# Storing the turned halves of x pair by pair, and two buffers for the gathered rows, in an attention and mixture-of-experts kernel

## The chip, the cores and the metric

The kernel runs on one core of one Trainium2 chip. The time is device microseconds of one execution; three executions of the kernel before were timed, and one more was profiled. PE is the matrix engine (TensorE), DVE the vector engine, ACT the scalar engine, POOL is GpSimd, SP issues most DMAs. A pair is two attention heads of one batch; there are 16 pairs, four for each of four batches.

## The reference

```python
def _attn_ref(q, k, v, centroids):          # q, k, v: 4 x 8 x 768 x 64
    q_assign = argmax(normed q . normed centroids)      # 16 clusters a head
    k_assign = argmax(normed k . normed centroids)
    mask = q_assign[:, :, :, None] == k_assign[:, :, None, :]
    scores = np.where(mask, scale * np.matmul(q, k.T), -1e9)
    ...
    return np.matmul(softmax(scores), v)

def _moe_ref(x, w_gate, w_noise, noise, w1, w2):        # x: 3072 x 512, 8 experts, F = 1024
    noisy_logits = x @ w_gate + log1p(exp(x @ w_noise)) * noise
    top2, top2_w = two largest a row, softmax of the two
    for e in range(E):
        for k in range(2):
            mask = top2[:, k] == e
            out[mask] += top2_w[mask, k, None] * (np.maximum(x[mask] @ w1[e], 0) @ w2[e])

x = attn_out.transpose(0, 2, 1, 3).reshape(B * S, H * D)   # attention's output is the experts' input
```

## The kernel before

One program does both parts. Attention goes pair by pair; a pair has 12 steps, and a hand-written table `AT` with due times in steps says where in that sequence every smaller piece of work is put. `at(step, f, ...)` files a piece under a third of a step; the loop over `t` in `attention` then calls, for each step, the pieces of the first third, `scores`, `split_p`, the second third, `values`, and the last third. The order in which Python calls them is the order of each engine's instructions: every engine works through its own list in order, and waits by semaphores.

In a step PE makes scores (L518), ACT takes the exponent (L519, tile `pe`), POOL splits it (L530, tile `pl`; for the last pairs DVE does that), and PE multiplies with v (L547 to L553). Beside it run, for the pairs behind, the maxima over keys (`b_max`: PE L487, DVE L490) and the cluster choice (DVE L425 to L442, the last of which writes the one-hot tile `oh`; PE turns it at L451, ACT makes the mask `mk`, SP places it). All PE results of this kind go through the PSUM tile `ring` with 6 buffers. `values` ends with DVE writing the pair's columns of the batch's output `xt` (L558 to L561; L558 reads `am`, L561 reads `rs`).

When the four pairs of a batch are done, two things happen for the whole batch within some five steps. `g_logits` and `g_logits2` turn `xt` on PE (L606), copy it on ACT (L608), multiply it with the gate's weights (L616) and copy that (L617); `g_turn` (PE L627, DVE L628) and `g_gate`, a chain of small DVE operations, choose the two experts of each token, and `g_list` writes the token into the table of its expert. And `store_x`, three times for two of the six token groups each, splits `xt` into two half-precision parts (ACT L598, then DVE L599 with two inputs in SBUF) in tile `xh`, which has one buffer, and SP stores them to `xs` in DRAM (L600): 128 pieces of 4 KB. For the last batch these calls stand in `experts`, between pieces of the first expert's first layer.

`experts` takes eight experts with up to 832 tokens each, in seven tiles of 128 (the last of 64). `gather_x` (POOL, L1128) fetches a tile of rows of `xs`; `turn_x` (SP, L1137, a DMA transpose) turns it into `xT`, of which there is one buffer. `layer1` is PE L1146, with ACT L1032 and L1034 and DVE L1035 behind it, `layer2` PE L1183 (L1174 and L1177 for the last tile), and POOL scatters the result (L1196). Expert 0 starts with the tokens of the first three batches (four tiles, part A); its other three tiles (part Bs) come when the last batch has been gated (`l_hot`, `l_sum`) and stored. With `late=1` all eight column blocks of its `layer1` stand behind `g_turn`: four inside the gate's chain, four beside `l_hot`, `l_sum`, `split_w2` and `store_x`. In the later experts `gather_x` of the next expert's tiles 0 to 3 stands in front of `layer1`, and all of its turns, with the gathers of tiles 4 to 6, in `tail`, between the pieces of `layer2`. SP also loads the weights (`stg`, 7 buffers) in the order of its list.

Memory in SBUF is laid out by pool; within a pool each tile lies behind the one that was asked for before it, all buffers of a name together. Pool `mo` (the experts') is opened when attention's pools `wk` and `fix` are closed and starts where `wk` began; a tile waits for the last use of each tile that lay in its place. `wk` holds, in this order and in bytes a partition, each rounded up to 32: `mm` 2 x 48, `nt` 2 x 512, `am` 3 x 48, `pe` 6 x 3,072, `vv` 3 x 6,240, `pl` 5 x 1,536, `rs` 2 x 24, `xm`; `fix` lies behind it and begins with `A0`. `mo` holds `xT` 13,312, `hT` 24,576, `hE` 2,048, `w2t` 16,384, three lists (448, 224 and 224), and then the smaller tiles.

## Time and profile before

| | us |
|---|---|
| median of three runs | 1095.08 (1093.82 to 1095.15) |
| profiled execution, its own time | 1094.86 |
| its span, first to last instruction | 1092.6 |
| PE busy in it | 1013.3 (93%) |

The profile is a page with shares of busy time, a list of waits and DMA issues, and views of any stretch. A timeline row gives start, duration, engine, line, operation, tiles, and in brackets the idle time in front of it with what ended that. In the page's second part each digit is the busy share of one of 40 equal slices.

### The profile page before, as it was taken

To read this page: it belongs to the slowest core of one execution; us is meant where nothing else is said; L and a number is where in the kernel's file an instruction comes from. 1 tells how busy PE (TensorE), PEld (TensorE's weight loads), DVE (VectorE), ACT (ScalarE), POOL (GpSimd) and SP (SyncE) were. 2 spreads that over 40 slices of the span, in tenths; PEclk is the share of its full clock that TensorE was granted. 3 is DMA by queue.
4 is the path that set the end of the run, shared out by engine and by line. 5 is a ranking of instruction groups with operands and counts; after the bars stand their busy time and mean duration, and the time that the engine had idled before them with its cause. 6 is when DMAs were issued, how large, how long until landed. Compare 5 with 4: busy or idle time off the path is not lost.

```text
span 1092.6 us, 22148 instructions
## 1 busy us (share of the span) xinstructions
PE 1013.3 (93%) x8518; PEld 685.8 (63%) x8518; DVE 687.4 (63%) x1455; ACT 512.0 (47%) x1046; POOL 549.1 (50%) x598
## 2 busy tenths in 40 slices
PE   5789998999899998988998999999999999999994
PEld 4678896889778896875444545545455454554542
DVE  5787676887768786897836554556445564455511
ACT  3467766767576766665512523315223152241510
POOL 9267673789766893872143434224352343423211
PEclk9899998999999999999999999999999999999998
DMA  7776765666755663505078484473844748445200
GB/s 197 172 186 145 175 159 167 144 173 144 196 142 137 168 157 95 158 10 157 39 233 202 126 194 162 104 212 117 201 144 102 216 117 205 140 102 164 59 33 33
DMA packets 143247, 158.08 MB, mean 145 GB/s; under 512 B 68857, under 2 KB 120441, under 8 KB 143138
## 3 DMA queue, kind: packets, MB, share of 16 engines
q1 hardware_dynamic: 129842, 120.25, 43.5%
q0 software_dynamic: 13296, 36.38, 10.9%
q8 instruction: 68, 1.11, 0.4%
q14 instruction: 41, 0.34, 0.1%
HBM read 78.21 MB, written 26.51 MB: 96 GB/s over the span
## 4 chain that ended last, share of the span: by engine, by line
PE 63%; DVE 13%; issue 8%; DMA 7%; POOL 4%; SPq 2%; ACT 2%; POOLq 0%; DVEq 0%; ACTq 0%
PE ring L1146 19%; PE ring L1183 17%; PE ring L518 8%; PE ring L487 4%; DMA A<-mk 2%; DVE aux L490 2%; PE av L547 2%; PE av L553 2%; PE av L549 2%; DVE mm L490 2%; DMA xs<-xh 1%; PE ring L406 1%; PE ring L385 1%; DVE pl L530 1%; DVE xh L599 1%
## 5 line engine op out<-in xcount | busy, mean ns | idle before, releaser
L530 POOL TENSOR_TENSOR pl<-pe 128x768 f16<-128x768 f32 x173 | 253.4, 1479 | 102.5 <-ACT pe L519 100.0
L1146 PE MATMUL ring<-xT,w1t 128*128 128x416 f16 (+2 forms) x1536 | 274.8, 340 | 2.0 <-DMA xT<-xg 2.0
L1183 PE MATMUL ring<-w2t,hT 128*128 128x512 f16 x1152 | 253.8, 381 | 2.2 <-ACT w2t L1038 1.2
L519 ACT ACTIVATE pe<-ring,l 128x384 f32<-128x384 f32 x384 | 201.5, 578 | 66.9 <-PE ring L518 62.0
L1146 PEld LDWEIGHTS <-w1t 128*128 128x128 f16 x1536 | 149.9, 98 | 121.2 <-issue 4.6
L1183 PEld LDWEIGHTS <-hT 128*128 128x128 f16 x1152 | 112.7, 98 | 137.0 <-issue 4.9
L1032 ACT ACTIVATE hr<-ring 128x416 f32<-128x416 f32 (+2 forms) x128 | 66.6, 520 | 276.4 <-PE ring L1146 269.1
L1196 POOL DMA_INDIRECT out<-yo,idx x52 | 62.7, 1207 | 173.1 <-DVE yo L1192 112.9
L490 DVE TENSOR_REDUCE aux<-ring 128x1 f32<-128x384 f32 x192 | 107.9, 562 | 60.8 <-PE ring L487 53.5
L518 PE MATMUL ring<-A 128*128 128x384 f32 x384 | 142.0, 370 | 1.0 <-ACT pe L519 0.7
L1035 DVE TENSOR_TENSOR hT<-hr,hT 128x416 f16<-128x416 f32 (+3 forms) x128 | 71.5, 560 | 101.0 <-ACT hT L1034 90.2
L518 PE MATMUL ring<-B 128*128 128x384 f32 x384 | 130.0, 339 | 1.5 <-DMA B<-nt 1.5
L1128 POOL DMA_INDIRECT xg<-xs,idx x52 | 54.6, 1050 | 145.0 <-DMA xT<-xg 120.4
L487 PE MATMUL ring<-A 128*128 128x384 f32 x384 | 108.8, 357 | 17.1 <-ACT pe L519 6.9
L1192 DVE SCALAR_TENSOR_TENSOR yo<-ring,we,xt 128x512 f32<-128x512 f32 (+1 forms) x49 | 36.7, 748 | 124.3 <-PE ring L1183 103.9
L490 DVE TENSOR_REDUCE mm<-ring 128x1 f32<-128x384 f32 x192 | 105.0, 547 | 0.0
L547 PE MATMUL av<-vv,pe 128*128 128x65 f16 x1152 | 98.0, 195 | 1.8 <-DVE xt L561 1.2
L549 PE MATMUL av<-vv,pe 128*128 128x64 f16 x1152 | 97.0, 193 | 0.0
L547 PEld LDWEIGHTS <-pe 128*128 128x128 bf16 x1152 | 80.1, 99 | 17.3 <-issue 12.6
L487 PEld LDWEIGHTS ring<-A 128*128 128x128 f32 x384 | 69.4, 190 | 30.5 <-ACT pe L519 13.6
L549 PEld LDWEIGHTS <-pe 128*128 128x128 bf16 x1152 | 78.5, 99 | 0.4
L518 PEld LDWEIGHTS ring<-A 128*128 128x128 f32 x384 | 73.3, 191 | 2.7 <-ACT pe L519 1.2
(206 smaller groups left out, 1412.8 us busy)
## 6 DMA issues: line engine op xcount, KB each, us to landing
stg<-in_moe_w SPq DMA_DIRECT2D x64, 512.0 KB
A<-hl SPq DMA_DIRECT2D x30, 384.0 KB
B<-hl SPq DMA_DIRECT2D x30, 384.0 KB
vt<-in_v SPq DMA_DIRECT2D x8, 768.0 KB
out<-zt SPq DMA_DIRECT2D x12, 512.0 KB
xs<-xh SPq DMA_DIRECT2D x12, 512.0 KB
A<-hl SPq DMA_DIRECT2D x60, 96.0 KB
B<-hl SPq DMA_DIRECT2D x30, 192.0 KB
```

The lines of the kernel that those rows point to most:

```text
L487: nc.tensor.matmul(t, A[:, 0, s, j * 128:j * 128 + 128], A[:, 1, s, n * 384:n * 384 + 384], start=True, stop=True)
L490: nc.vector.tensor_reduce(o, t, axis=X, op=OP.max, negate=True)
L518: nc.tensor.matmul(t, M[:, 1 - qi, s, ks], M[:, qi, s, ns], start=not qi, stop=bool(qi))
L519: nc.scalar.activation(pe[:, n], t, AF.Exp, bias=self.l64[:, 0:1], scale=self.scale)
L530: (nc.vector if last else nc.gpsimd).tensor_tensor(lo, pe, hi, op=OP.subtract)
L547: nc.tensor.matmul(av[:, j, :], ph[:, js], vv[:, hh, kj, 64:129], start=(kc == 0 and j == 0), stop=False, skip_group_check=True)
L549: nc.tensor.matmul(av[:, j, :64], ph[:, js], vv[:, hh, kj, 0:64], start=False, stop=False, skip_group_check=True)
L1032: nc.scalar.activation(r[:, :n], p, AF.Relu, scale=2.0 ** -HT)
L1035: nc.vector.tensor_tensor(h1, r[:, a:b], h0, op=OP.subtract)
L1146: nc.tensor.matmul(p, self.w1t[:, wi, c, f * 128:f * 128 + 128], self.xT[:, xi, c, n0:n1], start=(i == 0), stop=(i == 3 * ND - 1))
L1183: nc.tensor.matmul(p, self.hT[:, hi, f, t * 128:t * 128 + 128], self.w2t[:, wi, f], start=(i == 0), stop=(i == 3 * NF - 1))
L1196: i = nc.gpsimd.indirect_dma_start(out=self.out, out_offset=bass.IndirectOffsetOnAxis(ap=en[:r], axis=0), in_=yo[:r], in_offset=None, boun ...
```

## The change

`store_x` now takes one pair's 128 columns of all six token groups, and is called for each pair soon after its last `values`: pieces of 768 columns instead of 1024, 16 instead of 12, stored as 768 pieces of 512 B. `xs` keeps a row for each token; within a row the halves now alternate in blocks of 128 columns. The pieces of pairs 0 to 12 are in attention, those of 13 to 15 in `experts`. `xT` gets two buffers and is first asked for in `turn_x`, so behind `hT`, `hE`, `w2t` and the lists in pool `mo`. Turns 0 to 3 of the next expert and gathers 4 to 6 move from `tail` into `layer1` of the expert in front (`prep_x`); for expert 1 the first four gathers move in front of the last part-A `layer2`. `late` is gone: column block 0 of expert 0's `layer1` stands in front of `g_logits`, and each `split_w2` of expert 0 one place earlier.

```diff
@@ attention @@
+            if p <= NP - 4:
+                at(w + 37 + L + (6 if p == 0 else 0), self.store_x, p)
...
-                for c in range(3):
-                    at(z + 1.333 + 1.333 * c, self.store_x, b, c)
@@ store_x @@
-        h = pool.tile([128, n, 2, self.DM], F16, name="xh")
-        x, s = self.xt[b][:, n * c:n * c + n], self.sx[:, b:b + 1]
+        h = pool.tile([128, NJ, 2, 128], F16, name="xh")
+        x, s = self.xt[b][:, :, 128 * c:128 * c + 128], self.sx[:, b:b + 1]
         self.nc.scalar.activation(h[:, :, 0], x, AF.Copy, scale=s)
         self.nc.vector.scalar_tensor_tensor(h[:, :, 1], x, s, h[:, :, 0], op0=OP.mult, op1=OP.subtract)
-        self.nc.sync.dma_start(rap(self.xs, b * 128 * W + V * c, [[W, 128], [1, V]]), h.rearrange("p j i c -> p (j i c)"))
+        self.nc.sync.dma_start(rap(self.xs, b * 128 * NJ * W + 256 * c, [[NJ * W, 128], [W, NJ], [1, 256]]),
+                               h.rearrange("p j i c -> p j (i c)"))
@@ experts @@
-        self.xT = mo.tile([128, 2, ND, CAP], F16, name="xT")
+        self.xT = {}
...
         for c in range(4):
             self.max_w2(0, c)
+        self.layer1(0, 0, [A])
         for j in range(NJ):
             self.g_logits(b, j)
...
-        if not late:
-            self.layer1(0, 0, [A])
         self.g_turn(b)
...
-        f = 0 if late else 1
+        f = 1
...
+        self.split_w2(0, 0)
         self.l_hot(0)
...
-            self.split_w2(0, i)
             if i < 3:
-                self.store_x(b, i)
+                self.split_w2(0, i + 1)
+            if i:
+                self.store_x(self.NP - 4 + i)
...
                 for i in range(TA, T):
                     self.turn_x(0, i)
+                for i in range(4):
+                    self.gather_x(1, i)
...
             self.prep_w2(1, f - 5)
+            self.prep_x(1, f - 3)
             self.layer1(0, f, [Bs])
...
                     self.prep_w1(e + 1, f - 3)
+                    self.prep_x(e + 1, f - 3)
                 self.layer1(e, f, [(0, n), (n, CAP)])
...
+    def prep_x(self, e, i):
+        if 0 <= i < 4:
+            self.turn_x(e, i)
+            if i + 4 < self.T:
+                self.gather_x(e, i + 4)
@@ tail @@
-        done = 0
+        done = 4
...
-                while done < T and done < (t + 3 if e else 4 * (t - t0 + 1)):
-                    self.turn_x(n, done)
-                    if done + 4 < T:
-                        self.gather_x(n, done + 4)
-                    done += 1
+            while n < E and done < min(T, (t if e else 2 * (t - t0)) + 5):
+                self.turn_x(n, done)
+                done += 1
@@ turn_x @@
+        if t == 0:
+            self.xT[e] = self.mo.tile([128, ND, 2, self.CAP], F16, name="xT", bufs=2)
```

## Rows read from the trace of the kernel before

**Rows 1.** The table of stretches (busy time of each engine, granted clock of PE as a share of full speed, DMA share, GB/s): the end of attention and the last batch's logits, the way to the second expert, experts 1 to 7.

```profile
506.40:516.05 9.65, 8.03 (x83) 4.92 (x80) 6.62 (x10) 4.88 (x12) 0.00 (x0) 0.82 0.70 117
516.05:596.70 80.65, 74.36 (x399) 38.13 (x397) 48.80 (x110) 27.63 (x56) 26.38 (x32) 0.98 0.54 144
596.70:1044.00 447.30, 447.30 (x2342) 227.20 (x2343) 235.02 (x388) 153.75 (x327) 159.57 (x224) 1.00 0.53 147
```

**Rows 2.** The same table for single pairs: the first pairs of batches 1 and 2 (in which the batch before is stored and its logits are made) with a mid-batch pair between them, and two shorter stretches after the ends of batches 0 and 2.

```profile
156.30:197.30 41.00, 36.36 (x434) 30.75 (x433) 25.02 (x58) 26.03 (x54) 18.90 (x14) 0.92 0.60 163
...
250.70:275.70 25.00, 24.33 (x322) 22.90 (x319) 19.34 (x46) 18.13 (x38) 24.04 (x26) 1.00 0.63 153
275.70:316.50 40.80, 34.21 (x434) 28.77 (x432) 26.71 (x58) 25.83 (x53) 22.92 (x20) 1.00 0.60 163
...
176.00:187.80 11.80, 9.11 (x89) 7.05 (x90) 6.02 (x12) 8.21 (x17) 2.94 (x2) 0.71 0.28 102
...
421.50:433.50 12.00, 11.10 (x132) 9.05 (x133) 8.24 (x19) 8.96 (x21) 3.96 (x4) 0.86 0.17 57
```

**Rows 3.** The view of the tile `xh`: the operations that write and store it (shortest, median and longest in ns), and what ACT waited for in front of its part.

```profile
L598 ACT ACTIVATE xh<-xt,sx x12: 1143/1147/1150, 167.5 to 543.7; 128x1024 f16<-128x1024 f32 x12
L599 DVE SCALAR_TENSOR_TENSOR xh<-xt,sx,xh x12: 1265/1284/3866, 168.9 to 544.9; 128x1024 f16<-128x1024 f32 x12
...
  DMA xs<-xh: 19.6, 8
```

**Rows 4.** The timeline of PE behind the three batch ends: the pieces with the long idle times, and two groups of the same four turns, one early and one late.

```profile
178.63 0.90 PE L385 MATMUL ring<-ident,qk 128*128 128x128 f32 x3 [3.65 <-ACT lg L617]
...
181.03 1.12 PE L606 MATMUL ring<-ident,xt 128*128 128x128 f32 x4
...
184.37 0.66 PE L606 MATMUL ring<-ident,xt 128*128 128x128 f32 x4
...
298.20 0.55 PE L385 MATMUL ring<-ident,qk 128*128 128x128 f32 x3 [2.57 <-ACT lg L617]
...
304.49 0.44 PE L487 MATMUL ring<-A 128*128 128x384 f32 x1 [2.11 <-ACT pe L519]
...
422.37 0.45 PE L487 MATMUL ring<-A 128*128 128x384 f32 x1 [1.72 <-ACT pe L519]
```

**Rows 5.** The timelines of POOL and of DVE around the first store of batch 1.

```profile
286.44 2.89 POOL L530 TENSOR_TENSOR pl<-pe 128x768 f16<-128x768 f32 x2
...
289.37 1.46 POOL L530 TENSOR_TENSOR pl<-pe 128x768 f16<-128x768 f32 x1
...
288.60 3.32 DVE L599 SCALAR_TENSOR_TENSOR xh<-xt,sx,xh 128x1024 f16<-128x1024 f32 x1
```

**Rows 6.** POOL, DVE and PE in a mid-batch pair, about the step in which the change puts a pair's store; then POOL and DVE at the same place of two others, the first and the last of the nine pairs of this kind.

```profile
261.68 2.90 POOL L530 TENSOR_TENSOR pl<-pe 128x768 f16<-128x768 f32 x2
...
261.86 0.56 DVE L442 TENSOR_TENSOR oh<-ring,km 128x384 bf16<-128x384 f32 x1
262.34 0.56 DVE L490 TENSOR_REDUCE aux<-ring 128x1 f32<-128x384 f32 x1
...
263.58 0.52 PE L487 MATMUL ring<-A 128*128 128x384 f32 x2
...
115.52 1.47 POOL L530 TENSOR_TENSOR pl<-pe 128x768 f16<-128x768 f32 x1 [0.34 <-PE av L553]
...
115.58 0.56 DVE L442 TENSOR_TENSOR oh<-ring,km 128x384 bf16<-128x384 f32 x1
...
445.63 2.90 POOL L530 TENSOR_TENSOR pl<-pe 128x768 f16<-128x768 f32 x2
...
447.40 0.56 DVE L442 TENSOR_TENSOR oh<-ring,km 128x384 bf16<-128x384 f32 x1
```

**Rows 7.** What SP's own queue waited for between 480 and 520 us (total, times, longest), SP's timeline there, and DVE's at the end of attention.

```profile
SPq L1137 <- DVE rs L558: 8.4, 1, 8.4
...
507.54 5.51 SPq L1137 DMA_TRANSPOSE xT<-xg  x4
...
507.67 0.62 DVE L561 TENSOR_TENSOR xt<-av,rs 128x192 f32<-128x192 f32 x2
```

**Rows 8.** PE's timeline there: the first logits, the first `layer1`.

```profile
508.09 1.13 PE L606 MATMUL ring<-ident,xt 128*128 128x128 f32 x5 [1.23 <-DVE xt L561]
...
515.89 2.75 PE L1146 MATMUL ring<-xT,w1t 128*128 128x512 f16 x12
```

**Rows 9.** The chain that ended last (start, us, what), between 535 and 597 us: the second and third store of the last batch, the gather behind them, the last turn for expert 1.

```profile
540.98 2.63 DMA xs<-xh
...
546.20 2.61 DMA xs<-xh
...
549.66 3.45 DMA xg<-xs,idx
...
593.36 3.21 DMA xT<-xg
```

**Rows 10.** PE's timeline: the first `layer2` calls of expert 0, and the wait for expert 1.

```profile
546.90 0.38 PE L1183 MATMUL ring<-w2t,hT 128*128 128x512 f16 x1 [1.21 <-ACT w2t L1038]
548.22 18.47 PE L1183 MATMUL ring<-w2t,hT 128*128 128x512 f16 x77 [0.94 <-DVE w2t L1039]
...
596.70 1.55 PE L1146 MATMUL ring<-xT,w1t 128*128 128x416 f16 x5 [2.01 <-DMA xT<-xg]
```

More of the change, by code (lines that the diff above doesn't have):

```diff
@@ L27 @@
 AT = dict(
-    late=1,
     first={'place': -2.333, 'sims': [-3.333, -2.667], 'sum': [-2.333, -2.333], 'max1': -2.333, 'ge': -2.333, 'max2': -2.333, 'eq': -1.333, 'mask': -1.0, 'bmask': -1.0, 'ky': -2.333, 'split': [-5.333, -5.0, -5.333, -4.0], 'bmax': [3.667, 22.667], 'bstep': [1.0, 0.667], 'neg': [9.0, 26.667], 'negT': [9.333, 27.333]},
@@ L590, in zero_out, with store_x @@
                                self.zt[:, None, :].to_broadcast([128, 2 * DM // W, W]))
-    def store_x(self, b, c):
-        n = self.NJ // 3
-        W, V = 2 * self.NJ * self.DM, 2 * n * self.DM
-        pool = self.pre if b + 1 < self.B else self.mo
-        h = pool.tile([128, n, 2, self.DM], F16, name="xh")
-        x, s = self.xt[b][:, n * c:n * c + n], self.sx[:, b:b + 1]
+    def store_x(self, p):
+        b, c = divmod(p, self.H // 2)
+        NJ, W = self.NJ, 2 * self.DM
+        pool = self.pre if p <= self.NP - 4 else self.mo
+        h = pool.tile([128, NJ, 2, 128], F16, name="xh")
+        x, s = self.xt[b][:, :, 128 * c:128 * c + 128], self.sx[:, b:b + 1]
         self.nc.scalar.activation(h[:, :, 0], x, AF.Copy, scale=s)
         self.nc.vector.scalar_tensor_tensor(h[:, :, 1], x, s, h[:, :, 0], op0=OP.mult, op1=OP.subtract)
-        self.nc.sync.dma_start(rap(self.xs, b * 128 * W + V * c, [[W, 128], [1, V]]), h.rearrange("p j i c -> p (j i c)"))
+        self.nc.sync.dma_start(rap(self.xs, b * 128 * NJ * W + 256 * c, [[NJ * W, 128], [W, NJ], [1, 256]]),
+                               h.rearrange("p j i c -> p j (i c)"))
     def g_logits(self, b, j):
@@ L828, in experts @@
         Bs = (TA * 128, CAP)
-        late = AT["late"]
         for t in range(TA):
@@ L928, in tail @@
         n = e + 1
-        if n < E:
-            if e == 0:
-                for t in range(min(4, T)):
-                    self.gather_x(n, t)
-        done = 0
-        for t in range(t0, T):
-            if n < E:
-                while done < T and done < (t + 3 if e else 4 * (t - t0 + 1)):
-                    self.turn_x(n, done)
-                    if done + 4 < T:
-                        self.gather_x(n, done + 4)
-                    done += 1
+        done = 4
+        for t in range(t0, T):
+            while n < E and done < min(T, (t if e else 2 * (t - t0)) + 5):
+                self.turn_x(n, done)
+                done += 1
             self.layer2(e, t)
@@ L1002, in extra @@
                                                  bounds_check=self.N - 1, oob_is_err=False)
-                    nc.sync.dma_start_transpose(self.xT.rearrange("p i c n -> p (i c) n")[:, :, 0:128], xg)
+                    nc.sync.dma_start_transpose(self.xT[E - 1].rearrange("p c i n -> p (c i) n")[:, :, 0:128], xg)
                     for f in range(NF):
@@ L1009, in extra @@
                                 nc.tensor.matmul(p, self.w1t[:, wi, c, f * 128:f * 128 + 128],
-                                                 self.xT[:, xi, c, 0:128], start=(i == 0), stop=(i == 3 * ND - 1))
+                                                 self.xT[E - 1][:, c, xi, 0:128], start=(i == 0), stop=(i == 3 * ND - 1))
                                 i += 1
@@ L1136, in turn_x @@
         xg = self.xg.pop((e, t))
-        nc.sync.dma_start_transpose(self.xT.rearrange("p i c n -> p (i c) n")[:, :, t * 128:t * 128 + r], xg[:r])
+        if t == 0:
+            self.xT[e] = self.mo.tile([128, ND, 2, self.CAP], F16, name="xT", bufs=2)
+        nc.sync.dma_start_transpose(self.xT[e].rearrange("p c i n -> p (c i) n")[:, :, t * 128:t * 128 + r], xg[:r])
     def layer1(self, e, f, parts):
@@ L1146, in layer1 @@
                     nc.tensor.matmul(p, self.w1t[:, wi, c, f * 128:f * 128 + 128],
-                                     self.xT[:, xi, c, n0:n1], start=(i == 0), stop=(i == 3 * ND - 1))
+                                     self.xT[e][:, c, xi, n0:n1], start=(i == 0), stop=(i == 3 * ND - 1))
                 i += 1
```

## The prediction

> **What bounds the kernel now.** I first read the table of stretches. From 596.7 to 1044 us PE is busy all of the time at full clock [rows 1]: nothing there can be won by bringing rows earlier, and whatever the second `xT` buffer and the moved turns do to experts 2 to 7 is worth nothing. What can be won lies in front: PE idles 1.6 + 6.3 = 7.9 us between the end of attention and expert 1 [rows 1], and in attention the pair that follows a batch end takes some 41 us where a mid-batch pair takes 25 [rows 2]. The extra 16 us hold the logits' work, but also 4.6 and 6.6 us without any PE work where the ordinary pair has 0.7. The tile view of `xh` says what that is: ACT stood 19.6 us, in 8 pieces, waiting for a store of `xh` to land [rows 3], since there is one buffer. PE's timeline shows who paid [rows 4].
>
> **Batch ends: a gain.** A pair's store leaves one piece at the batch end instead of three; the next user of `xh` comes twelve steps later, so no one waits for a landing. PE's idle pieces behind the second and third store vanish: 3.65 (batch 0), 2.57 + 2.11 (batch 1), 1.72 (batch 2), together 10.05 us [rows 4]. After two of them PE ran at half clock: a granted 0.71 of 11.8 us is 6.8 us at half, 0.86 of 12 us is 3.4 us [rows 2], and the same four turns took 1.12 us at 181 and 0.66 us at 184 [rows 4]. Of the first 6.8 us about 1.4 fell into the idle piece, so 5.4 us at half cost 2.7; of the second some 0.8, so 1.3 us are lost. With the idle time gone I count this as gone too. Gain: 10.05 + 4.0 = 14.0 us. Ends: 9 (new waits behind ACT's logit copies, the clock not won) to 18 (2 x 1.15 us of ACT and 2 x 1.28 us of DVE less at each end [rows 3] help as well).
>
> **Ordinary pairs: a loss.** Ten stores now stand in pairs that had none. By size each is 3/4 of the old: ACT 0.87, DVE 0.96 us [rows 3]. ACT's part is hidden: a mid-batch pair has ACT busy 18.1 of 25 us [rows 2]. DVE's part is not so simple. L599 usually takes 1.28 us, but 3.87 at worst [rows 3]. At 288.60 it took 3.32 us: POOL was in `pl` until 289.33 and again from 289.37 to 290.83, and DVE ended 1.1 us after POOL had paused [rows 5]. So L599 waits until POOL rests, and every DVE instruction behind it waits too. In the new place it stands right behind L442. In the mid-batch pair L442 ends at 262.42 and POOL works until 264.58 [rows 6]: 2.2 us. Behind it in DVE's list are the L490 that free `ring`. From the tile of the first L490 (262.34) PE takes mask, two scores and one L487 tile before the second L487 tile, some 0.2 us after 263.58, needs that buffer again. It would be free at 262.42 + 2.2 + 0.96 + 0.56 = 266.1 less the 0.2 us by which L599 begins early, some 2.2 us late: PE loses what L599 waits. In the first and last of the nine pairs read in this way POOL rests at 116.99, 0.85 after L442, and at 448.53, 0.57 after [rows 6]; over all nine the waits are 0.6 to 2.3 us, 11.7 in sum. The tenth store (pair 0, moved six steps on) has no row; I leave it in the rounding. PE catches a part up, having 0.7 us of slack in 25 [rows 2]; I take 7/10: 8.2 us. Ends: 0 (all caught up) to 12.7.
>
> The SBUF page of the Trainium skill ("SBUF: two separate sides") says that a DVE operation with two SBUF inputs and a GpSimd operation that reads SBUF exclude each other for one whole instruction, and that the one which starts first has its way. By that DVE would come in after the POOL instruction that is running. The trace agrees on the exclusion (3.32 against 1.28 us), but there DVE was passed over by a second `pl` [rows 5]. What the page would give is the third rival.
>
> SP issues each store in front of the mask's placement (step 17 against 18), and the mask is read from step 21.3 on; I cost this at nothing, up to 1 us a pair if the store delays the mask.
>
> **Start of the experts: a loss.** `layer1(0, 0)` now stands in front of the logits in PE's list, and needs all four first turns. Where those may start follows from the places in SBUF. Before, `xT` lay at the start of `wk`, over `am`, and the first turn waited 8.4 us for L558, the last reader of `am` [rows 7]. Now 24,576 + 2,048 + 16,384 + 896 = 43,904 bytes lie in front of it, so its first buffer runs from 43,904 to 57,216; `rs` begins at 128 + 1,024 + 192 + 18,432 + 18,720 + 7,680 = 46,176, inside it. The last reader of `rs` is L561, ending at 508.29 [rows 7]. Four turns take 5.5 us to issue [rows 7] and the last lands 3.2 us after its own issue [rows 9], so at 508.4 + 4.2 + 3.2 = 515.8; by the other bound, PE at 515.89 not held up with a first turn at 507.54 [rows 7, 8], up to 516.8. I take 516.3. PE idles from 506.4, where it used to begin the logits at 508.09 and finish them at 515.9 [rows 8]. Then come 2.65 us of `layer1` and 8 us of logits: the gate starts at 526.9 instead of 516, 10.9 later, with 2.65 us of work done.
>
> Behind that PE wins 0.94 + 1.21 us, for `split_w2` stands earlier [rows 10], and about 1.3 of the 2.01 us for expert 1's rows [rows 10], since only turns 5 and 6 are left behind the late weight load. It loses 0.5 (`l_hot` behind a `split_w2`). The three last stores start one place later, some 5 us, beside the 10.9. Before, store to store took 5.22 us, and the gathers started at 549.66 [rows 9]; turns landed near 559, 7.5 us before PE asked at 566.7 [rows 10]. The landing of 768 pieces of 512 B has no row: 2.0 (2.6 by bytes [rows 9]) to 5.2 (twice); I take 3.2, near the turns' 3.21. So they land near 559 + 10.9 + 5 + 0.5 = 575.4, and PE asks near 571.4: 4 us lost (0 to 7.5). Sum of PE's idle time in this stretch: 7.9 - 1.23 [rows 8] - 2.15 - 1.3 + 9.9 + 0.5 + 4 = 17.6, so +9.7 us (5 to 15). The clock there is 0.82 and 0.98 [rows 1] with idle pieces in it already; I leave it as it is. The moved gathers and turns cost POOL and SP issues only, in stretches where PE is full [rows 1]; that cover gone, one late turn would cost its 3.2 us an expert.
>
> **Sum**, on the profiled execution's 1094.86 us: -14.0 + 8.2 + 9.7 = +3.9, so 1098.8 us. The profiled execution stands 0.2 us under the median of 1095.08, which I leave out.
>
> **Rivals.** First, faster: L599 finds POOL resting, or the pairs catch up. The place is DVE behind L442 in ten pairs; for it speaks that DVE is busy 19.3 of 25 us there, against it that POOL is busy 24.0 [rows 2]. At 1 us for all ten stores the time is 1094.86 - 14.0 + 1 + 9.7 = 1091.6, and 1088 if the turns for part Bs come in time too. It decides below 2.1 us for all ten, where the sum passes -2.2. Second, worse: with 9.9 us idle PE restarts at half clock for 6.8 us, as after batch 0's end (3.4 us lost), and part Bs waits 7.5 instead of 4: 1105.7. Third, no change: DVE gets in after the running `pl` alone. Then the nine waits are 7.1 in sum (0.7 instead of 2.2 in the pair of rows 6, the first and last unchanged), 7/10 of them 5.0, and the time 1095.6. This is the skill's rule as mentioned above. To the same place leads a first turn that does not wait for L561; some 4 us earlier, it would give 1094.8.
>
> **How the numbers follow.** Forecast 0.40, its own range 1097 to 1103; worse 0.11; no change 0.23; faster 0.26. About 0.2%, or 2.2 us, is what a measurement of this kernel can tell from no change. Faster: 0.26 + 0.02 of the third. Same: 0.21 of the third + 0.03 from the forecast's lower end. Slower: 0.37 + 0.11. Range 1088 to 1106: it reaches to the faster case with its better end and to the worse one.
>
> **What would show it.** Right: ACT no longer idle in front of L598 in attention; pairs after batch ends near 36 us; L599 at 1 to 3 us in ordinary pairs, with an idle piece of PE in front of an L487; PE idle near 10 us in front of the first L1146, released by a turn, and idle again in front of part Bs. Wrong: L599 always near 1 us, the first L1146 earlier than the last `xt` plus 7 us, or any idle time of PE in experts 2 to 7.

## The result and the profile after

The changed kernel takes 1105.84 us (median of 4 runs, 1104.38 to 1108.79) where the kernel before took 1094.52 on the same chip: 1.0107 of it, with a 95% interval of 1.0083 to 1.0131. So it is slower, by some 11 us; the forecast was 3.9 us. The profiled execution took 1104.83 us with a span of 1103.0. In the changed kernel attention's lines have numbers one less (L598 to L600 are L597 to L599, L490 is L489, L561 is L560), `layer1` is L1151, the turn L1142.

The table of stretches, with the columns of [rows 1, 2] (us; busy time of PE, PEld, DVE, ACT, POOL with counts; granted clock; DMA share; GB/s): the pairs behind the ends of batches 0 and 1 with a mid-batch pair between them, the start of the experts up to the first `layer1` of expert 1, and experts 1 to 7.

```profile
163.30:197.10 33.80, 33.20 (x434) 28.93 (x433) 22.51 (x56) 23.59 (x52) 18.27 (x14) 1.00 0.65 162
253.40:282.10 28.70, 25.82 (x323) 24.27 (x320) 22.14 (x46) 18.99 (x38) 27.49 (x29) 0.94 0.61 147
282.10:316.00 33.90, 33.32 (x434) 29.00 (x433) 22.60 (x56) 23.55 (x51) 20.56 (x17) 1.00 0.64 162
...
506.80:608.30 101.50, 82.97 (x475) 42.95 (x475) 52.55 (x117) 31.71 (x68) 26.47 (x31) 0.92 0.49 121
608.30:1054.60 446.30, 446.16 (x2346) 226.92 (x2345) 237.43 (x390) 153.71 (x328) 161.03 (x226) 1.00 0.58 148
```

The pairs behind batch ends went from 41 to 33.8 us and PE idles 0.6 us in them [rows 2]. The mid-batch pair went from 25.0 to 28.7 us, with 2.9 us idle in the place of 0.7; a granted 0.94 of 28.7 us also means 3.4 us of it at 1.2 GHz in the place of 2.4, which the pair of before did not have. Up to expert 1 PE idles 18.5 us, where it was 7.9 before; experts 1 to 7 are full, as before [rows 1].

The tile `xh` (ns shortest, median, longest), and what ACT waited for in front of its part; the eight waits of [rows 3] are gone but for two, both behind attention:

```profile
L597 ACT ACTIVATE xh<-xt,sx x16: 930/933/974, 101.8 to 560.6; 128x768 f16<-128x768 f32 x16
L598 DVE SCALAR_TENSOR_TENSOR xh<-xt,sx,xh x16: 1005/1676/3131, 102.8 to 561.5; 128x768 f16<-128x768 f32 x16
...
  DMA xs<-xh: 7.5, 2
```

The timelines of ACT, DVE, POOL and PE at the place of [rows 6], in the mid-batch pair of the table (start, us, engine, line; in brackets the idle time in front and what ended it):

```profile
262.36 0.93 ACT L597 ACTIVATE xh<-xt,sx 128x768 f16<-128x768 f32 x1
...
264.58 0.56 DVE L441 TENSOR_TENSOR oh<-ring,km 128x384 bf16<-128x384 f32 x1
265.05 3.10 DVE L598 SCALAR_TENSOR_TENSOR xh<-xt,sx,xh 128x768 f16<-128x768 f32 x1
268.07 0.55 DVE L489 TENSOR_REDUCE aux<-ring 128x1 f32<-128x384 f32 x1
...
264.44 2.89 POOL L529 TENSOR_TENSOR pl<-pe 128x768 f16<-128x768 f32 x2
...
263.82 0.44 PE L486 MATMUL ring<-A 128*128 128x384 f32 x1 [0.85 <-ACT pe L518]
...
268.69 0.44 PE L486 MATMUL ring<-A 128*128 128x384 f32 x1 [2.03 <-DVE aux L489]
```

DVE's op, 1.0 us long by itself, stands until POOL's second `pl` is done at 267.33, the L489 behind it frees `ring` late, and PE idles 2.03 us. The 0.85 us belong to ACT: its half stands in front of the exponent (whether they cost anything, e5 tells). Behind the batch end of batch 1 the same op finds POOL at rest, and here POOL waits for DVE (its `pl` takes 1.92 us, not 1.46):

```profile
294.49 1.01 DVE L598 SCALAR_TENSOR_TENSOR xh<-xt,sx,xh 128x768 f16<-128x768 f32 x1
...
294.91 1.92 POOL L529 TENSOR_TENSOR pl<-pe 128x768 f16<-128x768 f32 x1 [1.31 <-PE av L552]
```

At the start of the experts SP's waits and PE's timeline answer to [rows 7, 8]:

```profile
SPq L1142 <- DVE xt L560: 9.6, 1, 9.6
```

```profile
516.27 4.05 PE L1151 MATMUL ring<-xT,w1t 128*128 128x512 f16 x12 [9.48 <-DMA xT<-xg]
...
578.26 2.02 PE L1151 MATMUL ring<-xT,w1t 128*128 128x320 f16 x7 [6.00 <-DMA xT<-xg]
```

In sum, from the two traces: attention ends at 506.50 before and at 506.79 after, and from there to the end the kernel takes 586.1 and 596.2 us. So the whole loss shows behind attention, but attention hides two large numbers of opposite sign, which the table under the experiments takes apart.

### The profile page after: what moved, and what is told of

It is laid out like the page before. It is cut to its first block, busy times and chain, and to the rows that moved or that the text cites. A ratio compares the mean times of both kernels' runs of the same rounds, so it can differ in the third digit from the quotient of the medians.

```text
span 1103.0 us, 22170 instructions
## 1 busy us (share of the span) xinstructions
PE 1011.9 (92%) x8518; PEld 685.2 (62%) x8518; DVE 695.9 (63%) x1459; ACT 510.9 (46%) x1050; POOL 553.4 (50%) x598
## 4 chain that ended last, share of the span: by engine, by line
PE 65%; DVE 10%; issue 8%; DMA 6%; POOL 6%; SPq 2%; ACT 2%; POOLq 0%; DVEq 0%; ACTq 0%
PE ring L1151 20%; PE ring L1188 17%; PE ring L517 8%; PE ring L486 5%; PE av L546 2%; PE av L552 2%; PE av L548 2%; DVE xh L598 2%; DMA A<-mk 2%; PE ring L405 2%; DMA stg<-in_moe_w 1%; DVE aux L489 1%; PE ring L384 1%; POOL tbl L781 1%; PE ring L606 1%
## 5 line engine op out<-in xcount | busy, mean ns | idle before, releaser
L1151 PE MATMUL ring<-xT,w1t 128*128 128x416 f16 (+2 forms) x1536 | 277.2, 342 | 15.6 <-DMA xT<-xg 15.5
L1151 PEld LDWEIGHTS <-w1t 128*128 128x128 f16 x1536 | 150.6, 99 | 136.6 <-issue 18.5
L489 DVE TENSOR_REDUCE aux<-ring 128x1 f32<-128x384 f32 x192 | 107.8, 561 | 66.1 <-PE ring L486 60.5
L517 PE MATMUL ring<-A 128*128 128x384 f32 x384 | 142.6, 371 | 1.0 <-ACT pe L518 0.7
L486 PE MATMUL ring<-A 128*128 128x384 f32 x384 | 112.3, 363 | 27.2 <-DVE aux L489 10.9
L489 DVE TENSOR_REDUCE mm<-ring 128x1 f32<-128x384 f32 x192 | 105.1, 547 | 0.0
L486 PEld LDWEIGHTS ring<-A 128*128 128x128 f32 x384 | 70.1, 191 | 43.8 <-DVE aux L489 15.0
L546 PEld LDWEIGHTS <-pe 128*128 128x128 bf16 x1152 | 80.3, 99 | 18.1 <-issue 11.7
```

What stands on the lines that cost most here:

```text
L486: nc.tensor.matmul(t, A[:, 0, s, j * 128:j * 128 + 128], A[:, 1, s, n * 384:n * 384 + 384], start=True, stop=True)
L489: nc.vector.tensor_reduce(o, t, axis=X, op=OP.max, negate=True)
L517: nc.tensor.matmul(t, M[:, 1 - qi, s, ks], M[:, qi, s, ns], start=not qi, stop=bool(qi))
L546: nc.tensor.matmul(av[:, j, :], ph[:, js], vv[:, hh, kj, 64:129], start=(kc == 0 and j == 0), stop=False, skip_group_check=True)
L1151: nc.tensor.matmul(p, self.w1t[:, wi, c, f * 128:f * 128 + 128], self.xT[e][:, c, xi, n0:n1], start=(i == 0), stop=(i == 3 * ND - 1))
```

## The experiments

On the chips of the experiments the kernel before took 1087 to 1100 us from run to run, so each result is given as a ratio to it, on the same chip, with its interval. The table takes attention apart (us; a pair goes from its first exponent to the next pair's). Ordinary pairs are those with a store of the change in them but no batch end: 1 to 3, 5 to 7, 9 to 11 and 13, with pair 2 apart; the pairs behind batch ends are 4, 8 and 12. Each row is one profiled execution. The nine pairs took 249.0 to 251.9 us in the five profiles with both halves at their new places (changed, e1, e9, e11, e12): their idle time is the same there (20.7 to 21.3 us), but one to three stretches of 3.4 us at half clock fall into them. They took 233.0 to 234.3 us in before, e3, e4, e5, e7 and e8.

| kernel | pair 2 | nine other ordinary pairs | three behind batch ends |
|---|---|---|---|
| before | 27.8 | 234.3 | 122.0 |
| changed | 32.5 | 249.0 | 101.5 |
| e3, neither half | 27.9 | 234.1 | 100.5 |
| e5, ACT's half alone | 29.6 | 234.0 | 100.7 |
| e6, DVE's op alone | 32.1 | 247.1 | 101.4 |
| e10, DVE's op alone, one input in PSUM | 32.3 | 238.9 | 101.4 |
| e9, store behind the mask | 29.1 | 249.5 | 101.5 |

**e1: `layer1(0, 0)` back behind the logits.**

```diff
-        self.layer1(0, 0, [A])
         for j in range(NJ):
             self.g_logits(b, j)
...
-        f = 1
+        f = 0
```

> The changed kernel with layer1(0, 0) moved back behind the logits and g_turn, as in the kernel before; everything else of the change stays. Theory: the idle time of 9.5 us in front of the first layer1 is the loss of the last stage, and the logits can cover the first turns again. Then attention's end stays at 506.4 us, that idle piece goes to under 2 us, and the time falls by 8 to 10 us, to 1096 to 1098 us. Rival: the idle piece only moves, because the stores behind the gate and the turns for part Bs set the time of this stage anyway. Then the idle time in front of part Bs grows by what the first piece loses and the time stays above 1102 us.

1095.81 us, 1.0019 [0.9999, 1.0039]. From attention's end on it takes 585.9 us, 10.3 less than the changed kernel and as before. PE's timeline: the first `layer1` and part Bs.

```profile
518.59 1.67 PE L1150 MATMUL ring<-xT,w1t 128*128 128x512 f16 x7 [1.04 <-DMA xT<-xg]
...
569.75 2.57 PE L1150 MATMUL ring<-xT,w1t 128*128 128x320 f16 x12 [3.95 <-DMA xT<-xg]
```

The theory holds: the place of `layer1(0, 0)` is the loss of this stage, and the other parts of the change (two `xT` buffers, moved gathers, turns and splits) come to nothing together.

**e2: DVE's op in `store_x` with one SBUF input.**

```diff
+        if p <= self.NP - 4:
+            self.nc.vector.tensor_scalar(h[:, :, 1], x, s, None, op0=OP.mult)
+        else:
             self.nc.vector.scalar_tensor_tensor(h[:, :, 1], x, s, h[:, :, 0], ...)
```

> The changed kernel, but in the pairs of attention (stores of pairs 0 to 12) DVE writes x times its scale into the low half, from one SBUF input, instead of x times its scale less the high half from two; so the low halves of these rows are left out and the values are wrong. ACT's part and the store stay. Theory: in the ordinary pairs DVE stands 1 to 2 us a pair waiting for POOL because it has two SBUF inputs. Then its op in store_x takes under 1.1 us in all pairs, the ordinary pairs lose 8 to 13 us less and the time is 1093 to 1098 us. Rival: the loss comes from ACT's part and from the store in SP's queue, and DVE only stands in a gap. Then the op gets shorter, but the time stays within 3 us of the changed kernel (1103 to 1108).

1102.55 us, 1.0082 [1.0056, 1.0108]. The op got shorter at rest and still stood in the ordinary pairs:

```profile
L599 DVE TENSOR_SCALAR xh<-xt,sx x13: 608/1662/2753, 102.5 to 441.5; 128x768 f16<-128x768 f32 x13
```

So the theory's condition fell: it takes no second SBUF input for DVE to stand behind POOL. The run takes no wait away and decides nothing on the cost of one. Its nine pairs take 244.1 us, 4.9 less than in the changed kernel, with an op 0.4 us shorter at rest and no stretch at half clock.

**e3, e5, e6: neither half, ACT's alone, DVE's alone.** In pairs 0 to 12; the store's place and its pieces stay.

```diff
+        if p <= self.NP - 4:
+            # e3: store a constant tile; e5: d = ACT's half; e6: d = DVE's op on x and a constant tile
+            self.nc.sync.dma_start(rap(self.xs, ...), ...)
+            return
```

> The changed kernel, but for pairs 0 to 12 neither ACT nor DVE splits x: the store, at the same place in SP's queue and with the same pieces of 512 B, writes a constant tile instead. The split of these rows is left out and the values are wrong. Theory: ACT's and DVE's parts are nearly all of the ordinary pairs' loss of 20.6 us, the store in SP's queue little of it (some 3 us, in the pair in which the mask came late). Then the time is 1085 to 1090 us. Rival: the stores delay the mask's placement in every pair. Then the time stays above 1097 us, with POOL or PE waiting for the tile mk in ordinary pairs.

> The changed kernel, but for pairs 0 to 12 ACT's half alone is made and stored (in 512 B pieces as before, the low half filled from the same elements); DVE's op in store_x is left out in these pairs, and the values are wrong. It goes with the next kernel: leaving out both parts moved attention's end by 21 us. Theory: DVE, which stands 1 to 2 us a pair until POOL rests, holds the larger part of that, some 12 us, and ACT's 0.93 us in front of the exponents some 8. Then attention ends near 494 us and the time is 1092 to 1096 us. Rival: ACT's part is the larger one, 15 us or more. Then attention ends at 501 us or later and the time is above 1099.

> The changed kernel, but for pairs 0 to 12 DVE's op alone is made and stored, with a constant tile in SBUF as its second input, so that it has two SBUF inputs as before and does not wait for ACT; ACT's half is left out in these pairs, and the values are wrong. Theory: DVE still waits for POOL and keeps some 12 of the 21 us; the recurring idle piece of 0.85 us in front of the exponents goes with ACT's part. Then attention ends near 498 us and the time is 1096 to 1100 us. Rival: DVE's wait was only there because ACT gave it its input late; then the op takes near 1 us in ordinary pairs, attention ends near 488 us and the time is under 1091.

e3: 1086.16 us, 0.9927 [0.9902, 0.9952]. e5: 1087.65, 0.9960 [0.9936, 0.9983]. e6: 1104.27, 1.0093 [1.0063, 1.0123]. The mid-batch pair in the three traces, in this order:

```profile
243.20:268.20 25.00, 24.33 (x324) 22.87 (x321) 19.37 (x46) 18.11 (x37) 24.00 (x26) 1.00 0.69 168
```

```profile
245.90:270.80 24.90, 24.05 (x322) 22.85 (x319) 19.25 (x45) 18.88 (x39) 23.89 (x26) 1.00 0.68 169
```

```profile
252.00:279.20 27.20, 24.47 (x323) 22.91 (x320) 22.20 (x46) 18.16 (x38) 26.02 (x28) 1.00 0.64 155
```

Without the halves the ordinary pairs are as before: the store's bytes cost nothing. With ACT's half alone the nine pairs are as before too; with DVE's op alone they keep 12.8 of 14.7 us. PE's idle pieces behind ACT's half are there in e5 too (7.9 us in front of L486 in the nine pairs, 1.7 before), but PE then waits 4.3 us less for `oh` at L450, and nothing is lost. My split of 12 to 8 was wrong: DVE's part is nearly all.

**e10: the same DVE op with one input in PSUM.** As e6, but from `aux[:, 500:512]` and a constant tile.

> The changed kernel, but for pairs 0 to 12 the op in store_x is made by DVE alone from other data: as many elements, at the same place in DVE's list, written to xh in SBUF, with one input from PSUM (twelve columns of aux, repeated) and the other a constant tile in SBUF; ACT's half is left out, and the values are wrong. It goes with the kernel in which DVE's op alone stayed, with two SBUF inputs: attention ended 2.5 us from that of the changed kernel, and the time was 1104.3. Theory: the cost of DVE's op is not its work but its standing until POOL rests, which goes with inputs that all lie in SBUF, for DVE's other ops in these pairs read PSUM and run beside POOL. Then the op takes near 1 us in all thirteen pairs, attention ends near 490 us, and the time is 1086 to 1092 us. Rival: DVE's list is full there and any op of this size costs the same, with POOL or without. Then attention ends after 500 us and the time stays above 1099.

1095.45 us, 1.0030 [1.0007, 1.0053]. The tile `xh`, then DVE and POOL in the mid-batch pair:

```profile
L602 DVE SCALAR_TENSOR_TENSOR xh<-aux,sx,jp x13: 1007/1009/1019, 101.7 to 435.6; 128x768 f16<-128x768 f32 x13
```

```profile
261.84 1.01 DVE L602 SCALAR_TENSOR_TENSOR xh<-aux,sx,jp 128x768 f16<-128x768 f32 x1
...
261.19 2.90 POOL L529 TENSOR_TENSOR pl<-pe 128x768 f16<-128x768 f32 x2
```

Now the op takes 1.01 us in all thirteen pairs, here in the midst of POOL's `pl`. The nine pairs fall by 247.1 - 238.9 = 8.2 us: that is the price of standing behind POOL, with 1.7 us in it for a stretch of 3.4 us at half clock that e10 does not have. But 238.9 - 234.3 = 4.6 us stay, the price of 1 us more in DVE's list, and attention ends at 494.36, not near 490: both theory and rival had a part of it.

**e9: the store behind the mask in SP's queue.**

```diff
+                at(w + 38.333 + L + (6 if p == 0 else 0), lambda: self.pend())   # the DMA alone
```

> The changed kernel, but the store's DMA of pairs 0 to 12 is issued 1.333 steps later, behind the mask's placement in SP's queue; ACT's and DVE's parts stay where they are. Theory: SP waits for DVE's late op with the mask queued behind it, and that cost 2.4 us in the pair in which the mask came late and little elsewhere; the time falls by 2 to 4 us, to 1101 to 1104. Rival: most of the ordinary pairs' loss goes through SP's queue, not through DVE's and ACT's own lists. Then attention ends 8 us or more earlier and the time is under 1098.

1102.08 us, 1.0088 [1.0054, 1.0121]. Pair 2 takes 29.1 us, 3.4 less; the nine others are unchanged. SP's rows of the changed kernel show which store it is: what SP waited for in pairs 1 and 2, the store of pair 0 (the one moved six steps on), and the mask of pair 2.

```profile
SPq L599 <- DVE aux L489: 3.8, 1, 3.8
```

```profile
104.41 0.59 SPq L599 DMA_DIRECT2D xs<-xh  x1
...
121.25 2.97 SPq L458 DMA_DIRECT2D A<-mk  x4
```

DVE's op for this store ran until 104.41. Behind the store SP's list has ten placements of `hl`, a store of zeros and two loads, and the first placement of the mask left at 121.25; in the kernel before it left at 117.76:

```profile
117.76 3.28 SPq L459 DMA_DIRECT2D A<-mk  x4
```

PE waited 2.4 us for it, 1.3 before. In e9 this store leaves at 111.85, behind the placements of `hl`, and PE waits for no mask in pair 2.

**e11, e12: another place for expert 0's `xT`.** e11 asks for a first `xT` and leaves it unused; e12 asks for `hr` first.

```diff
+        mo.tile([128, 512], F32, name="hr", bufs=3)      # e12, behind lsw and ahead of xT
```

> The changed kernel, but expert 0 takes the second of the two xT buffers: the first is asked for once more at the start and left unused. The second lies over A0's end and A1, which the last pairs give back before rs. Theory: the first turns waited for L561, the last reader of rs, because the first buffer lies over it; so now they start at the end of the gathers, several us earlier, the idle time in front of the first layer1 falls from 9.5 us to 1 to 4 us, and the time is 1096 to 1101 us. Rival: the turns wait for something else at the same time (the gathers of expert 0's rows, SP's list). Then the first turn still starts within 1.5 us of the last L561 and the time stays above 1103.

1104.67 us, 1.0103 [1.0072, 1.0134]. It says nothing on the theory: the unused buffer gave its place to expert 0's rows, which lay at 94,688 as in the changed kernel, and SP still waited 9.6 us for L560.

> The changed kernel, but the three tiles hr are asked for ahead of xT, so that expert 0's xT lies 6,144 bytes further on, from 100,832, behind rs (96,960 to 97,024) and over the last part of A0 and the front of A1. (The kernel in which a first xT was asked for and left unused changed nothing of this: expert 0's rows still lay at 94,688, over rs, and its time says nothing on the theory.) Theory: the first turn waited for L560 because xT lies over rs; now it waits for the last scores that read A0, some 8 us earlier, and then for the gathers, the last of which lands near 503.6. So the first turn starts before 504 us, the idle time in front of the first layer1 falls from 9.5 to 1 to 4 us, and the time is 1096 to 1100 us. Rival: the turns wait for something else that ends with attention, wherever xT lies. Then the first turn still starts within 1.5 us of the last L560 and the time stays above 1103.

1098.01 us, 1.0034 [1.0011, 1.0057]. SP's waits, its timeline and PE's:

```profile
SPq L1143 <- PE ring L517: 1.2, 1, 1.2
```

```profile
499.44 6.63 SPq L1143 DMA_TRANSPOSE xT<-xg  x4
```

```profile
508.85 4.87 PE L1152 MATMUL ring<-xT,w1t 128*128 128x512 f16 x12 [2.75 <-DMA xT<-xg]
```

The turns start 9 us earlier, and the stage takes 5.6 us less. That the first turn waits for the last reader of `rs` is shown.

**e4, e7, e8: what the batch end cost before.** All are the kernel before. e4 stores `x` in six pieces of 2 KB in two buffers; e7 issues the loads of `q` and `k` and the zeros six steps later, behind the stores; e8 is both.

```diff
-                for c in range(3):
-                    at(z + 1.333 + 1.333 * c, self.store_x, b, c)
+                for c in range(6):
+                    at(z + 0.667 + 0.667 * c, self.store_x, b, c)          # e4, e8; xh with bufs=2
...
-                    at(w + T["qk"] + 24 * g + (T["qf"] if (b, g) == (0, 1) else 0), self.load_qk, b, g)
+                    at(... else 6 if b and not g else 0), self.load_qk, b, g)    # e7, e8; zero_out + 6
```

> The kernel before, with nothing of the change: x still stored at the batch end, but in six pieces of one j each (2 KB a partition) with two buffers of xh in the place of one of 4 KB, one every 0.667 of a step in the place of three every 1.333. Theory: the change's 20 us at the batch ends come from the waits on the single buffer of xh and from the idle time and the half clock that follow them, and not from the smaller work there. Then ACT waits under 4 us on xh in attention instead of 19.6, the pairs after batch ends take 34 to 37 us, and the time is 1077 to 1087 us. Rival: what the change won is the ACT and DVE work that left the batch end, or the landing of a store is so long that two buffers wait as one did. Then the pairs after batch ends stay at 39 to 41 us and the time at 1092 to 1097.

> The kernel before, with nothing of the change: only the loads of q and k that stand right in front of the batch end's stores (load_qk of g = 0 for batches 1 to 3) and the stores of zeros to out (zero_out) are issued six steps later, behind the stores of x. Theory: ACT waits for xh at a batch end because the store's bytes queue behind 2 MB of loads and zeros; so the waits of 7.7 to 9.6 us from store to store at the first two batch ends shrink to the 5.2 us that the third one, without a load in front, shows. Then ACT waits under 14 us on xh in attention and at the start of the experts, PE idles 4 to 7 us less in the pairs after the first two batch ends, and the time is 1084 to 1090 us. Rival: the waits are set by what stands on ACT and in SP's queue between two stores (logit copies, the mask's placement), or the loads that come later delay another transfer as much. Then the pairs after batch ends stay within 2 us of 41 us and the time stays within 3 us of the kernel before.

> The kernel before with the loads of q and k and the zeros moved behind the batch end's stores (which alone gave 0.53% and left ACT waiting 13.5 us on xh) and with x stored in six pieces with two buffers (which alone gave nothing, as the first store then still landed 7 us after its issue). Theory: the two go together: with the loads gone a 2 KB piece lands in some 3 us, and with two buffers the next ACT op does not wait for it; so ACT's waits on xh in attention fall under 4 us, the pairs after batch ends take 34 to 37 us, and the time is 1077 to 1083 us. Rival: the shorter pieces bring more ops and issues to the batch end, and these or the mask's placement set its length. Then the pairs after batch ends stay at 38 to 40 us and the time at 1086 to 1090.

e4: 1092.99 us, 0.9991 [0.9968, 1.0015]. e7: 1086.89, 0.9947 [0.9931, 0.9963]. e8: 1083.64, 0.9910 [0.9883, 0.9937]. The three pairs take 124.1, 115.1 and 115.5 us (122.0 before). Why e4 gave nothing stands in SP's and ACT's timelines:

```profile
166.05 0.61 SPq L589 DMA_DIRECT2D out<-zt  x1
166.71 0.72 SPq L327 DMA_DIRECT2D qk<-in_q  x1
167.47 1.28 SPq L327 DMA_DIRECT2D qk<-in_k  x1
169.23 9.62 SPq L600 DMA_DIRECT2D xs<-xh  x3
```

```profile
177.00 0.72 ACT L598 ACTIVATE xh<-xt,sx 128x512 f16<-128x512 f32 x1 [6.08 <-DMA xs<-xh]
```

The store's bytes stand behind 2 MB of loads and zeros; two buffers are full before the first has landed, near 177. e7 shows the cause: without the loads the first end's pair falls from 41.0 to 36.5 us, the other two by 0.8 and 1.7. e8 adds the buffers, which bring the three pairs nothing (115.5 against 115.1 us); what its profiled execution is ahead of e7's lies behind attention (581.9 against 585.2 us from attention's end). What is left in e8 is DVE behind POOL again, this time in front of L442 (DVE, POOL, PE):

```profile
285.68 4.09 DVE L599 SCALAR_TENSOR_TENSOR xh<-xt,sx,xh 128x512 f16<-128x512 f32 x1
...
287.75 1.46 POOL L530 TENSOR_TENSOR pl<-pe 128x768 f16<-128x768 f32 x1
...
290.29 0.51 PE L451 MATMUL ring<-identb,oh 128*128 128x128 bf16 x6 [2.78 <-DVE px L1060]
```

**e13 to e16: other places for stores and loads.** The six pieces start at step 2.0 (e13), 1.333 (e14, e15) or 0.667 (e16); the loads and zeros are six steps later in e13 and e14, nine in e15 and e16.

> The kernel before with the loads and zeros behind the batch end's stores and six pieces in two buffers, as in the kernel that gave 0.9%, but the first piece 1.333 of a step later (the others behind it at 0.667 as there). In that kernel the first or second DVE op of a batch end took 4.1 us in place of 0.74 at two of the three ends, since POOL had three pl in hand. Theory: DVE's wait for POOL sets the batch end too; started when POOL is nearly through, every op takes under 2 us, the pairs after batch ends lose 2 to 4 us each, and the time is 1074 to 1081 us. Rival: the batch end is set by the landing of the pieces and by ACT's list, and a later start only moves the end. Then the time stays within 2 us of 1083.6, or above.

> The kernel before with the loads and zeros behind the batch end's stores and six pieces in two buffers, the first piece at step 1.333 of the batch end: between the kernel that began at 0.667 (1083.6 us, its op of 4.1 us in front of L442 at two ends, with PE idle for 2.8 us behind it) and the one that began at 2.0 (1090.7 us, no op over 1.6 us, but the last pieces gave xt back so late that the pair behind took 2.5 to 3.3 us more). Theory: both costs are real and this start has little of either, because the first op stands behind L442 and the last piece ends two thirds of a step before xt is written again: the pairs after batch ends take 36 to 38 us, those behind them under 26.5, and the time is 1077 to 1082 us. Rival: ACT's and DVE's added work at the batch end is the limit, and a start in between only shares out the costs. Then the time is 1083 to 1089 us.

e13: 1090.71 us, 0.9975 [0.9952, 0.9999]. e14: 1090.40, 0.9989 [0.9966, 1.0012]. DVE's ops are short in e13 (831 ns median, 1516 at most), and still the three pairs take 116.9 us, and 117.4 in e14; the theories fall. The reading that `xt` came back too late falls too, by the tile `nt` of e14, what it kept waiting (us, times), and by PE's timeline there:

```profile
  PEld ring L518: 12.9, 4
  PE ring L518: 11.8, 4
```

```profile
195.38 0.69 PE L518 MATMUL ring<-B 128*128 128x384 f32 x1 [4.20 <-DMA B<-nt]
```

The moved loads now stood in front of the small DMA of `nt`; the wait was one that my own edit had made. In pairs 5 and 9 of e14 PE idles 2.3 us, as before; what they take more, 56.9 against 51.7 us, comes with 7.6 us of work at half clock.

> The kernel before with six pieces in two buffers, the first at step 1.333 of the batch end, and the loads and zeros moved by nine steps in the place of six. With six they stood right in front of the small DMA of nt in SP's queue: PE waited 12.9 us for nt in the kernel with this start (1.9 us in the kernel before), two pieces of it 4.0 and 4.2 us. Theory: that wait, not ACT's and DVE's added work, is what kept this start from paying; behind the placement of the next hl the loads meet no small DMA. Then PE waits under 4 us for nt, the pairs after batch ends and the pairs behind them lose those 4 us and the half clock that follows, and the time is 1076 to 1083 us. Rival: the added work sets the batch end, or the loads that come later delay the next qk or v. Then the time stays at 1086 or above.

> The same with the first piece at step 0.667: there DVE's op stood 4.1 us in front of L442 at two ends (PE idle 2.8 us) in the kernel with the loads moved by six (1083.6 us), where PE waited 5.5 us for nt. Theory: the wait for nt goes here too, DVE's op in front of L442 stays: 1078 to 1082 us, and 1 to 4 us above the kernel that starts at 1.333. Rival: as there; the time stays within 2 us of 1083.6 or goes above it.

e15: 1081.73 us, 0.9888 [0.9858, 0.9919]. e16: 1086.17, 0.9926 [0.9904, 0.9948]. In e15 the wait for `nt` is gone, and the three pairs are shorter:

```profile
  PEld ring L518: 1.8, 1
  PE ring L518: 1.5, 1
```

```profile
156.10:192.00 35.90, 34.12 (x434) 28.97 (x433) 26.47 (x61) 26.13 (x57) 18.39 (x14) 1.00 0.56 142
271.10:308.50 37.40, 34.06 (x434) 28.83 (x433) 28.32 (x61) 26.50 (x57) 23.22 (x20) 1.00 0.53 136
388.20:426.60 38.40, 35.50 (x434) 30.02 (x433) 29.73 (x61) 26.72 (x56) 23.18 (x21) 0.96 0.53 132
```

Moving the loads and zeros by nine steps in the place of six helps at this start; at step 0.667 it does not (e16 and e8 lie within each other's intervals). e15 is faster than the kernel before and the changed one, with none of the change in it. It pays a little of its gain back: in each of pairs 5 and 9 PE now waits 1.0 us for the loads themselves (54.2 us against 51.7).

## Why the prediction was right or wrong

The sign was right, the mechanisms that the prediction costed showed, the time lay 0.2 us inside the range, and the size was off by 7 us. The step that failed is the sum's second term, "Ordinary pairs: a loss", put at 8.2 us and measured at 281.5 - 262.1 = 19.4. By the runs it is made of

- DVE standing behind POOL, 8.2 us in the nine pairs (e6 less e10). Here the prediction was right: in the nine pairs that it read (2 to 13, without pair 1) the ops of the changed kernel take 20.8 us, 11.7 more than nine at 1.01, and it had 11.7 us of waits. That 7/10 of them, 8.2 us, is the measured cost to the tenth is chance: the 8.2 hold 1.7 us of half clock, and pair 1 in the place of pair 2.
- DVE's own microsecond, 4.6 us (e10 less before). The prediction set the op's own 0.96 us and the L490 behind it against the time until PE needs the buffer, in one pair, and so let PE lose "what L599 waits" and no more in all nine. How the 4.6 us arise is not shown: in e10 PE waits 1.1 us for L489 in the nine pairs, as for L490 before, and the mid-batch pair takes 25.3 us against 25.0. The most, 1.2 and 1.1 us, falls in pairs 5 and 9, in which DVE was busy 23.3 of some 25.8 us.
- ACT's half, 14.7 - 12.8 = 1.9 us beside DVE's op. "ACT's part is hidden" was read from ACT's busy share and holds for ACT's half alone (e5); how the two come to lose it together is not shown.
- Pair 2, 4.7 us, of which e9 gives back 3.4: a store in SP's queue delays the mask. The prediction named this for a pair's own store and costed it "at nothing, up to 1 us a pair"; it was the tenth store, that of pair 0, which it left "in the rounding".

**Batch ends**, 14.0 forecast, 122.0 - 101.5 = 20.5 measured. The third of the three pairs before, beside the two of [rows 2]:

```profile
395.80:435.90 40.10, 35.71 (x434) 29.90 (x433) 27.58 (x58) 26.01 (x53) 23.38 (x21) 0.96 0.50 127
```

PE idled 4.6 + 6.6 + 4.4 = 15.6 us in them and 1.8 in the changed kernel: 13.8 us, of which the prediction counted the four longest pieces, 10.05. The half clock, put at 4.0, cost some 4.4 by PE's rows. That ACT's waits for landings are part of it is shown by e7, which moves nothing but the loads and zeros and wins 6.9 of the 20.5 us; and the reason for the long landings, which the prediction had not looked for, by e4 and e7. The shorter work at the batch end, which the prediction left to its upper end of 18, is part of it too. How much is not settled: e15 recovers 10.3 of the 20.5 us with all of the work still there; PE idles some 8.0 us in its three pairs, and whether the rest is the work itself or a place that I have not found is open.

**Start of the experts**, 9.7 forecast, 596.2 - 586.1 = 10.1 measured, and by its own steps: 9.48 us idle in front of the first `layer1` (9.9 forecast), released by a turn that waited for L560, which e12 shows to come from the place over `rs`; 6.00 us in front of part Bs (4, at most 7.5); 18.5 us idle in all (17.6). The prediction's "PE asks near 571.4" does not follow from its terms: 566.7 + 10.9 - 2.65 - 2.15 + 0.5 = 573.3, which would leave 2.1 us lost and not 4. PE asked at 572.3, and the rows came at 578.3, not 575.4. The first `layer1` ran 4.05 us where it took 2.75 [rows 8], at a granted 0.67, PE having idled before it; the forecast left the clock as it was, and only its rival "worse" had this. The gaps at `layer2` of expert 0 [rows 10] are gone, as forecast.

The two errors of attention, +11.2 and -6.5, partly cancel; with +0.4 of the start and 1.3 us in the pairs 0, 14 and 15 (80.0 and 81.3 us), which differ as much from run to run (pair 0 takes 33.9 to 35.1 us in the five profiles named above), the forecast's 3.9 becomes 10.3, and the profiled executions lie 9.97 us apart.

**The rivals.** "Worse", 1105.7 us, comes nearest in time by luck: it put 9.7 + 3.4 + 3.5 = 16.6 us on the start of the experts, for half clock and a longer wait for part Bs, and that stretch measured 10.1. "Faster" fell with DVE's op at 1.6 to 3.1 us in ordinary pairs. "No change" rested on DVE coming in after the running `pl`, or on a first turn that does not wait for L561. The `pl` that ran when DVE's op began at 265.05 ended at 265.91, and DVE ended at 268.15, after a second one; and the first turn waited. The Trainium skill, SBUF — State Buffer, section "SBUF: two separate sides", has the one that starts first win and the other wait for the whole instruction. The trace agrees where DVE was first (POOL's 1.92 us at 294.91) and in that DVE waits for a running `pl`; it differs in that a DVE op that already waits is passed over by POOL's next op when that follows without a gap (3.10 us here in the place of 1.01; 4.09 in e8 in the place of 0.74). The page also counts one-input ops in a two-port mode among those that wait, and e2's op did wait (0.61 us at rest, 2.75 beside POOL), though no row names its mode; e2's theory had left that half of the rule out.

## What to carry to other kernels

Price an op that is moved into a full stretch three times: what it waits for at its new place, its own time in the list of its engine (nine ops of 1.01 us without a wait cost 4.6 us here, on an engine busy 19 of 25 us), and what stands behind its DMA in the queue. One pair read closely does not price the others. When a store's buffer is waited for, look in the DMA queue ahead of it before adding buffers: here 2 MB of loads made the wait, buffers alone won nothing (e4) and moving the loads alone 0.5% (e7), as long as no small awaited DMA fell behind them. Where a tile lies decides whom its first writer waits for; asking for another tile first can move it.

## What was not expected of the hardware

A DVE op with all its tensors in SBUF stands until POOL pauses, not until POOL's running op ends (768 columns: 1.01 us at rest, up to 3.13 in the changed kernel; 512 columns: 0.74 at rest, up to 4.12 in e8). The same op with one input in PSUM took 1.01 to 1.02 us in all 13 pairs, beside POOL's `pl` too.
